# Scaling the exponentials of a banded attention before they are turned, in place of the output after it

## The chip, the cores and the metric

The kernel runs on one core of a Trainium2 chip. The metric is the device time of one execution in microseconds. An execution under the profiler leaves a trace, and the views below are read from it.

## The reference, cut to what matters

```python
def _attn_ref(q, k, v, n_global, n_local):          # q, k, v: (4, 8, 768, 64)
    scores = scale * np.matmul(q, k.transpose(0, 1, 3, 2)) + bias
    scores = np.where(keep, scores, -1e9)            # 8 global keys, 96 local ones
    scores = scores - np.max(scores, axis=-1, keepdims=True)
    a = np.exp(scores)
    a = a / (np.sum(a, axis=-1, keepdims=True) + 1e-09)
    return np.matmul(a, v)

def _moe_ref(x, w_gate, w1, w2):                     # x: (3072, 512), the attention's output
    ...                                              # gate: exp of logits, 8 rounds of row and column scaling
    for e in range(8):
        out += P[:, e:e + 1] * (np.maximum(x @ w1[e], 0.0) @ w2[e])
```

The quotient `a / sum` is what the change computes in another place. Everything is float32; the kernel splits large operands into a high and a low part and multiplies three products for one.

## The kernel before, in words

The program has two stages. In the first, some 325 us long, the attention is computed for 32 **pairs** of heads (`n`; 4 batches by 2 halves of the sequence by 4 pairs). Four pairs make a **unit**; there are eight. A pair has three **groups** (`t = 3n + group`), each a query tile of 128 rows for both heads. Behind it, for some 1870 us, the experts run as large matmuls, in a form with seven products in place of eight.

`Banded.unit` steps through a unit two groups at a time. One such step is called a **chunk** here, six to a unit. The chunk writes TensorE's (PE's) instructions in this order, and PE keeps it:

1. `ahead`: scores of the two groups that come four groups later (`s_ps`), then `softmax` of them: VectorE (DVE) adds the bias and takes the row maximum into `p_sb` (L309), ScalarE (ACT) takes the exponential in place and the row sums (L313).
2. `flush`: the product with V (`o_ps`) of the two groups that were turned in the chunk before. When a pair ends here, `o_ps` is multiplied by `inv` on DVE (L404), and split into the parts `xh` (ACT, L405) and `xl` (DVE, L406) that the experts read.
3. `turn`, twice: PE transposes the exponentials of two groups into `t_ps`, and a copy takes them to `pT` (L336).
4. `between`: some 4 us of **filler**, the first expert's matmuls on units that are done (`h_ps`, `y_ps`, `g_ps`).
5. In two chunks of three `prepare`: PE transposes q and k of a later pair into two `tp` tiles; ACT casts them to `qh` and `kh` (L266), DVE subtracts to `ql` and `kl` (L267). In the third chunk `invert`, for two pairs: PE transposes `inv` into `r_ps`, and DVE copies that back to `inv` (L414).

The sums are handled by pair: after the third group ACT adds EPS to the six sums (L316), DVE takes reciprocals (L317), and ACT spreads each over 64 columns into the tile `inv` (L319).

From the second unit on, `t_ps`, `tp` and `r_ps` share two PSUM banks (tag `tp`), given out in turn: the first `t_ps` of a chunk takes the bank of the q transposes before it, the second that of the k transposes, once `ql` and `kl` have been read out of them. `s_ps` has one bank for each head of the pair.

GpSimd (POOL) adds and subtracts x tiles for the later stage (L607 to L611, tile `op`). All DMAs are issued in one queue on SyncE (SP): the loads of q, k and v (`raw_qk`, `raw_v`, `early`), and the spills of what POOL made (`op_m<-op`, L817). On PE and SP, as on the others, a scheduler that runs when the program is built fixes one order, except that the attention's and filler's PE instructions stay as written. The wait of an instruction holds up all that stands behind it on its engine or queue.

Of the kernel before, what the change touches and what calls it, by code (L numbers as in the profile page):

```python
# [8 lines left out]
F32 = mybir.dt.float32  # L9
# [3 lines left out]
ALU = mybir.AluOpType  # L13
# [4 lines left out]
P = 128  # L18
# [4 lines left out]
EPS = 1e-9  # L23
UT = 3
# [8 lines left out]
CHUNK = 2  # L33
LAG = 6
FG = 2
GROUPS = (((0, 0), (1, 0)), ((0, 1), (1, 1)), ((0, 2), (1, 2)))
# [78 lines left out]
class Banded:  # L115
# [154 lines left out]
    def scores(self, ts):  # L270
# [19 lines left out]
                    self.pe.matmul(s_ps, lhsT=t[m][0], rhs=t[m][1], start=(m == 0), stop=(m == 2))  # L290
        return s_lists

    def softmax(self, t, s_list):


        nc, D = self.nc, self.D
        n, group = divmod(t, len(GROUPS))
        _, half, g = self.work[n]
        p_sb = self.wrk.tile([P, 2, 2, P], F32, name="p_sb")
        mx = self.wrk.tile([P, 2], F32, name="mx", bufs=4)  # L300
        if group == 0:
            self.sums[n] = self.wrk.tile([P, UT, 2], F32, name="sm", bufs=4)
        sm = self.sums[n]
        views = []
        for u, (j, i) in enumerate(GROUPS[group]):
            h = 2 * g + j
            pv = p_sb[:, u, 0:len(KEYS[half][i])]
            views.append(pv)
            nc.vector.tensor_tensor_reduce(out=pv, in0=s_list[u], in1=self.bias(h, half, i), scale=-(D ** -0.5), scalar=3.0e38,  # L309
                                           op0=ALU.add, op1=ALU.min, accum_out=mx[:, u:u + 1])  # L310
        for u, pv in enumerate(views):
            j, i = GROUPS[group][u]
            nc.scalar.activation(out=pv, in_=pv, func=AF.Exp, bias=mx[:, u:u + 1], scale=-1.0,  # L313
                                 accum_out=sm[:, i, j:j + 1])
        if group == len(GROUPS) - 1:
            nc.scalar.add(sm, sm, EPS)  # L316
            nc.vector.reciprocal(out=sm, in_=sm)  # L317
            self.inv[n] = self.wrk.tile([P, UT, P], F32, name="inv", bufs=3)
            nc.scalar.copy(out=self.inv[n].rearrange("p t (j d) -> p (t j) d", j=2),  # L319
                           in_=sm.rearrange("p t j -> p (t j)").unsqueeze(2).broadcast_to([P, 2 * UT, D]))  # L320
        return p_sb
# [31 lines left out]
    def unit(self, u, xh, xl, between):  # L353

        NG, per = len(GROUPS), len(GROUPS) * (self.H // 2)
        if u == 0:
            self.load_qk(1)
            self.prepare(0)  # L360
            self.scale_bias(0)
            self.keep_warm(self.ps, "o", WARM0)
            self.ahead(range(0, CHUNK))
            self.load_v(2)
            self.prepare(1)
            for g in range(1, self.H // 2):
                self.scale_bias(g)
            for t in range(CHUNK, AHEAD, CHUNK):
                self.ahead(range(t, t + CHUNK))
            self.prepare(2)  # L370
        for t in range(u * per, (u + 1) * per, CHUNK):
            self.ahead(range(t + AHEAD, t + AHEAD + CHUNK))
            self.flush()
            for t1 in range(t, t + CHUNK):
                n, group = divmod(t1, NG)
                if group == 0:
                    self.outs[n] = self.ps.tile([P, UT, P], F32, name="o_ps", tag="o", bufs=2)
                g = n % (self.H // 2)
                self.pending.append((n, group, self.turn(t1), self.outs[n], xh[g], xl[g]))
            for c in (CHUNK, 1, 1):  # L380
                between(c)
            n = t // NG
            if t % (2 * NG) == CHUNK:
                self.invert(n)
                self.invert(n + 1)
            else:
                self.prepare(n + NG)
        self.idle = None

    def flush(self):  # L390


        ended = None
        for n, group, pT, o_ps, xh, xl in self.pending:
            self.values(n, group, pT, o_ps)
            if group == len(GROUPS) - 1:
                ended = n, o_ps, xh, xl
        self.pending = []
        if ended is None:
            return  # L400
        n, o_ps, xh, xl = ended
        if n % 2:
            self.load_v(n + 3)
        self.nc.vector.tensor_tensor(out=o_ps, in0=o_ps, in1=self.inv.pop(n), op=ALU.mult)  # L404
        self.nc.scalar.copy(out=xh, in_=o_ps)  # L405
        self.nc.vector.tensor_tensor(out=xl, in0=o_ps, in1=xh, op=ALU.subtract)  # L406

# [683 lines left out]
```

## Time and profile before

| | before |
|---|---|
| median of 3 runs | 2198.84 us (2198.79 to 2199.56) |
| the profiled execution's own time | 2199.65 us |
| its span, first to last instruction | 2197.9 us |
| PE busy | 2177.2 us, 99% of the span |
| DVE, ACT, POOL busy | 1329.1, 757.1, 1127.9 us |

The profile is of one execution; 1.75 us of its time lie outside the span. Busy matmuls are pipelined and overlap in the records, so a row's mean duration is longer than what one costs PE; the cost is the step from one start to the next.

### The profile page before, as it was taken

The page shows a single profiled execution, that of the slowest core. Times are in us where ns is not written, and L with a number is a line of the kernel's source. Part 1 is how long each engine was busy: PE and PEld are TensorE (multiplying, and loading weights), DVE is VectorE, ACT ScalarE, POOL GpSimd, SP SyncE. Part 2 cuts the span into 40 slices and gives each one's busy share as a digit, 9 for nine tenths or more (in the row PEclk, how much of TensorE's full clock was granted, in tenths as well). Part 3 has the DMA queues.
Part 4 walks back from the last instruction along what each step waited for, and adds up shares of the span by engine and source line. Part 5 has one row for each costly group of instructions (what it writes and reads, how often), then busy time and mean ns, then how long its engine had stood idle before and what let it go on. Part 6 is the DMA issues. An engine that isn't in the chain of part 4 may idle for free.

```text
span 2197.9 us, 29372 instructions
## 1 busy us (share of the span) xinstructions
PE 2177.2 (99%) x10851; PEld 1811.4 (82%) x10851; DVE 1329.1 (60%) x2348; ACT 757.1 (34%) x1540; POOL 1127.9 (51%) x1061
## 2 busy tenths in 40 slices
PE   7999999999999999999999999999999999999998
PEld 5888888888888888888888888888888888888887
DVE  6555546756656666665665665665566566566565
ACT  6677763322222222223232222222232223222231
POOL 5767565445445445445455554544454545545440
PEclk8999999999999999999999999999999999999999
DMA  5666553111111111171111111111611111111111
GB/s 122 162 194 175 144 165 128 48 58 48 49 58 48 55 51 48 58 259 50 57 48 58 48 49 58 49 51 55 201 57 49 49 58 49 58 48 49 58 39 50
DMA packets 207817, 173.47 MB, mean 79 GB/s; under 512 B 102704, under 2 KB 170800, under 8 KB 207664
## 3 DMA queue, kind: packets, MB, share of 16 engines
q1 hardware_dynamic: 207664, 171.51, 25.3%
q8 instruction: 87, 1.43, 0.3%
q14 instruction: 66, 0.54, 0.1%
HBM read 142.36 MB, written 29.10 MB: 78 GB/s over the span
## 4 chain that ended last, share of the span: by engine, by line
PE 97%; ACT 1%; DVE 1%; DMA 0%; SPq 0%; issue 0%; POOL 0%; ACTq 0%; DVEq 0%
PE y_ps L109 46%; PE bank_a L109 11%; PE bank_d L109 11%; PE bank_c L109 11%; PE bank_b L109 5%; PE h_ps L109 3%; PE o_ps L109 2%; PE s_ps L109 2%; PE t_ps L112 2%; PE tp L112 1%; PE r_ps L112 1%; PE g_ps L109 0%; ACT p_sb L313 0%; PE y_ps L705 0%; PE y_ps L704 0%; PE y_ps L703 0%
## 5 line engine op out<-in xcount | busy, mean ns | idle before, releaser
L990 DVE SCALAR_TENSOR_TENSOR early<-y_ps,pm,early 128x512 f32<-128x512 f32 x672 | 503.0, 749 | 241.8 <-PE y_ps L109 241.3
L563 POOL TENSOR_TENSOR wl<-wsum,wh 128x1280 fp32r<-128x1280 f32 x90 | 266.2, 2957 | 577.8 <-ACT wh L562 577.8
L585 POOL TENSOR_TENSOR wsum<-w1f 128x256 f32<-128x256 f32 x450 | 317.5, 740 | 319.1 <-DMA w1f<-in_moe_w_dram 319.1
L109 PE MATMUL y_ps<-w2h,h_set 128*128 128x512 f32 x1408 | 433.5, 389 | 0.0
L109 PE MATMUL y_ps<-w2h,x 128*128 128x512 f32 x1408 | 433.4, 389 | 0.0
L562 ACT CAST w2h<-w2f 128x1024 fp32r<-128x1024 f32 x90 | 94.8, 1054 | 688.6 <-issue 610.6
L109 PEld LDWEIGHTS y_ps<-w2h,h_set 128*128 128x128 f32 x1408 | 264.3, 188 | 54.9
L109 PEld LDWEIGHTS y_ps<-w2h,x 128*128 128x128 f32 x1408 | 264.3, 188 | 54.9
L109 PE MATMUL y_ps<-w2l,h_set 128*128 128x512 f32 x704 | 274.1, 389 | 0.1
L109 PE MATMUL y_ps<-w2l,x 128*128 128x512 f32 x704 | 273.9, 389 | 0.0
L109 PE MATMUL bank_a<-m,wh 128*128 128x512 f32 x696 | 242.8, 389 | 1.0 <-DVE h_set L635 1.0
L109 PE MATMUL bank_d<-x,wh 128*128 128x512 f32 x696 | 242.7, 389 | 0.0
L109 PE MATMUL bank_c<-x,wh 128*128 128x512 f32 x696 | 242.5, 389 | 0.0
L563 POOL TENSOR_TENSOR w2l<-w2f,w2h 128x1024 fp32r<-128x1024 f32 x90 | 216.0, 2400 | 48.5 <-ACT w2h L562 48.5
L675 DVE TENSOR_TENSOR early<-early,bank_d 128x512 f32<-128x512 f32 x90 | 62.0, 689 | 175.8 <-PE bank_d L109 171.8
L109 PEld LDWEIGHTS y_ps<-w2l,h_set 128*128 128x128 f32 x704 | 132.1, 188 | 27.8 <-DVE early L990 0.5
L109 PEld LDWEIGHTS y_ps<-w2l,x 128*128 128x128 f32 x704 | 132.1, 188 | 27.5
L109 PEld LDWEIGHTS bank_a<-m,wh 128*128 128x128 f32 x696 | 130.6, 188 | 29.0 <-DVE h_set L635 1.9
L109 PEld LDWEIGHTS bank_c<-x,wh 128*128 128x128 f32 x696 | 130.6, 188 | 27.1
L109 PEld LDWEIGHTS bank_d<-x,wh 128*128 128x128 f32 x696 | 130.6, 188 | 27.1
L109 PE MATMUL bank_a<-m,wl 128*128 128x512 f32 x348 | 135.4, 389 | 0.0
L109 PE MATMUL bank_d<-x,wl 128*128 128x512 f32 x348 | 135.4, 389 | 0.0
(233 smaller groups left out, 3480.8 us busy)
## 6 DMA issues: line engine op xcount, KB each, us to landing
w1f<-in_moe_w_dram SPq DMA_DIRECT2D x92, 512.0 KB, 3.5
w2f<-in_moe_w_dram SPq DMA_DIRECT2D x92, 512.0 KB, 3.4
x<-op_m SPq DMA_DIRECT2D x16, 512.0 KB, 7.6
op_m<-op SPq DMA_DIRECT2D x30, 256.0 KB, 2.8
m<-op_m SPq DMA_DIRECT2D x12, 512.0 KB, 7.2
out_dram<-early SPq DMA_DIRECT2D x24, 256.0 KB, 4.0
ys<-y_sb SPq DMA_DIRECT2D x21, 256.0 KB, 2.8
early<-ys SPq DMA_DIRECT2D x21, 256.0 KB, 4.1
```

Source lines behind the costliest of these rows:

```text
L109: return self.tc.keep_in_program_order(self.engine.matmul(*args, **kw))
L112: return self.tc.keep_in_program_order(self.engine.transpose(*args, **kw))
L562: self.nc.scalar.copy(out=hi, in_=full)
L563: self.nc.gpsimd.tensor_tensor(out=lo, in0=full, in1=hi, op=ALU.subtract)
L585: nc.gpsimd.tensor_tensor(out=s[:, n], in0=x, in1=y, op=op)
L675: tt(out=t3, in0=t3, in1=d, op=ALU.subtract)
L990: nc.vector.scalar_tensor_tensor(out=a, in0=y_ps, scalar=moe.pm[:, tt, e:e + 1], in1=a, op0=ALU.mult, op1=ALU.add)
```

## The change

For pairs 0 to 3 (`early_pair`) all stays. For the other 28, each group takes its two sums into a small tile of its own, adds EPS and takes reciprocals on DVE, and multiplies the exponentials in `p_sb` by them: in the first and third group one head on DVE and one on ACT, in the second both on ACT. `invert` with its transposes, the spread tile `inv` and the multiplication of `o_ps` are dropped for these pairs.

```diff
+    def early_pair(self, n):
+
+        return n < self.H // 2
...
-        if group == 0:
+        early = self.early_pair(n)
+        if not early:
+            sm = self.wrk.tile([P, 2], F32, name="sm2", bufs=8)
+        elif group == 0:
             self.sums[n] = self.wrk.tile([P, UT, 2], F32, name="sm", bufs=4)
-        sm = self.sums[n]
...
-                                 accum_out=sm[:, i, j:j + 1])
-        if group == len(GROUPS) - 1:
+                                 accum_out=self.sums[n][:, i, j:j + 1] if early else sm[:, u:u + 1])
+        if not early:
+            nc.vector.tensor_scalar(out=sm, in0=sm, scalar1=EPS, scalar2=None, op0=ALU.add)
+            nc.vector.reciprocal(out=sm, in_=sm)
+            for u, pv in enumerate(views):
+                if u == 0 and group != 1:
+                    nc.vector.tensor_scalar(out=pv, in0=pv, scalar1=sm[:, u:u + 1], scalar2=None, op0=ALU.mult)
+                else:
+                    nc.scalar.mul(pv, pv, sm[:, u:u + 1])
+        elif group == len(GROUPS) - 1:
+            sm = self.sums[n]
             nc.scalar.add(sm, sm, EPS)
             nc.vector.reciprocal(out=sm, in_=sm)
-            self.inv[n] = self.wrk.tile([P, UT, P], F32, name="inv", bufs=3)
+            self.inv[n] = self.wrk.tile([P, UT, P], F32, name="inv", bufs=2)
...
-            if t % (2 * NG) == CHUNK:
+            if t % (2 * NG) != CHUNK:
+                self.prepare(n + NG)
+            elif self.early_pair(n):
                 self.invert(n)
                 self.invert(n + 1)
-            else:
-                self.prepare(n + NG)
...
-        self.nc.vector.tensor_tensor(out=o_ps, in0=o_ps, in1=self.inv.pop(n), op=ALU.mult)
+        if self.early_pair(n):
+            self.nc.vector.tensor_tensor(out=o_ps, in0=o_ps, in1=self.inv.pop(n), op=ALU.mult)
```

Three places of the built order, before and now. The first is on PE, in the second unit, at the end of an `invert` chunk: filler (`h_ps`), the transposes of `inv` (`r_ps`), and the next chunk's scores. Before:

```order
L109 MATMUL h_ps<-x_194,w1h 128x384
L109 MATMUL h_ps<-x_192,w1l 128x384
L109 MATMUL h_ps<-x_192,w1h 128x384
L112 MATMUL r_ps<-ident,inv 128x128 x6
L109 MATMUL s_ps_1054<-kl,qh 128x256
L109 MATMUL s_ps_1055<-kl,qh 128x256
```

Now:

```order
L109 MATMUL h_ps<-x_194,w1h 128x384
L109 MATMUL h_ps<-x_192,w1l 128x384
L109 MATMUL h_ps<-x_192,w1h 128x384
L109 MATMUL s_ps_1073<-kl,qh 128x256
L109 MATMUL s_ps_1074<-kl,qh 128x256
```

The six transposes are gone here and at 13 more places; nothing else on PE moves, and the scores follow the filler.

The second is on DVE, at the 24th `prepare` (the one whose q transposes start at 211.07 us in the trace before): the subtractions `ql` and `kl` that free the two `tp` banks, and the four maxima (`ISA`, each with a read of its result) of the chunk behind them. Before:

```order
L406 TENSOR_TENSOR x_195<-o_ps,x_193 128x3x128
L317 RECIPROCAL sm<-sm 128x6
L267 TENSOR_TENSOR ql<-tp,qh 128x384
L267 TENSOR_TENSOR kl<-tp,kh 128x512
L309 ISA p_sb,mx<-s_ps_3505,early 128x256
L309 ISA mx 128x1
```

Now:

```order
L326 TENSOR_SCALAR p_sb<-p_sb,sm_3504 128x256
L267 TENSOR_TENSOR ql<-tp,qh 128x384
L315 ISA p_sb,mx<-s_ps_3589,early 128x256
L315 ISA mx 128x1
L315 ISA p_sb,mx<-s_ps_3589,early 128x256
L315 ISA mx 128x1
L315 ISA p_sb,mx<-s_ps_3590,early 128x256
L315 ISA mx 128x1
L315 ISA p_sb,mx<-s_ps_3590,early 128x256
L315 ISA mx 128x1
L267 TENSOR_TENSOR kl<-tp,kh 128x512
```

`kl` has moved behind the four maxima. It stands so at the 16th, 24th and 32nd `prepare`, and at no other from the third unit on. At the same place ACT's order ahead of the `qh` and `kh` casts was

```order
L405 CAST x_193<-o_ps 128x3x128
L862 COPY y_sb<-y_ps 128x512
L316 ACTIVATE sm<-sm 128x6
L266 CAST qh<-tp 128x384
L319 COPY inv<-sm 128x384
L266 CAST kh<-tp 128x512
```

and is now

```order
L351 COPY pT<-t_ps 128x512
L328 ACTIVATE p_sb<-p_sb,sm_3493 128x256 x2
L877 COPY y_sb<-y_ps 128x512
L328 ACTIVATE p_sb<-p_sb,sm_3504 128x256
L266 CAST qh<-tp 128x384
L266 CAST kh<-tp 128x512
```

Three scalings (L328) have come between; the EPS addition and the spread copy are gone, and the cast of x (L420 now) stands further ahead.

The third is on SP, at the loads of q and k for the 16th `prepare`. Before:

```order
L218 DMA raw_qk<-in_k_dram 32x2x64
L218 DMA raw_qk<-in_k_dram 96x2x64 x2
L218 DMA raw_qk<-in_k_dram 32x2x64
L218 DMA raw_qk<-in_k_dram 96x2x64
L218 DMA raw_qk<-in_k_dram 32x2x64
L817 DMA op_m_204<-op 256x1x512
L218 DMA raw_qk<-in_k_dram 128x2x64
```

Now:

```order
L218 DMA raw_qk<-in_k_dram 32x2x64
L218 DMA raw_qk<-in_k_dram 96x2x64 x2
L832 DMA op_m_204<-op 256x1x512
L218 DMA raw_qk<-in_k_dram 32x2x64
L218 DMA raw_qk<-in_k_dram 96x2x64
L218 DMA raw_qk<-in_k_dram 32x2x64
L218 DMA raw_qk<-in_k_dram 128x2x64
```

The spill of POOL's result has moved ahead of three loads; the last load (`128x2x64`) stands behind the same DMAs as before. At the 12th `prepare` the same kind of spill has moved ahead of two.

## Rows read from the trace of the kernel before

**Rows 1.** The page: share by engine of the chain that ended last.

```profile
PE 97%; ACT 1%; DVE 1%; DMA 0%; SPq 0%; issue 0%; POOL 0%; ACTq 0%; DVEq 0%
```

**Rows 2.** By stretch: PE, PEld, DVE, ACT, POOL busy (x), PEclk, DMA share, GB/s.

```profile
80.00:120.00 40.00, 38.87 (x331) 33.68 (x327) 20.84 (x79) 27.60 (x88) 38.04 (x39) 1.00 0.64 178
120.00:160.00 40.00, 40.00 (x343) 35.08 (x343) 21.53 (x78) 28.73 (x88) 25.39 (x31) 1.00 0.64 173
```

**Rows 3.** Waits of PE over the span, the longest: us, times, longest one.

```profile
PE s_ps L109 <- DVE kl L267: 4.3, 2, 3.2
```

**Rows 4.** Tile inv: ns min/median/max, first and last start, forms.

```profile
L414 DVE COPY inv<-r_ps x32: 546/557/559, 31.2 to 316.8; 128x384 f32<-128x384 f32 x32
L319 ACT COPY inv<-sm x32: 497/513/525, 21.9 to 309.5; 128x384 f32<-128x384 f32 x32
...
L404 DVE TENSOR_TENSOR o_ps<-o_ps,inv x32: 555/561/567, 34.0 to 322.4; 128x384 f32<-128x384 f32 x32
```

**Rows 5.** PE in order of time (start, us), at chunk ends with and without r_ps.

```profile
138.96 0.34 PE L109 MATMUL h_ps<-x,w1h 128*128 128x384 f32 x1
139.14 0.82 PE L112 MATMUL r_ps<-ident,inv 128*128 128x128 f32 x6
139.89 0.39 PE L109 MATMUL s_ps<-kl,qh 64*128 64x256 f32 x2
...
303.96 0.34 PE L109 MATMUL h_ps<-x,w1h 128*128 128x384 f32 x1
304.22 0.39 PE L109 MATMUL s_ps<-kl,qh 64*128 64x256 f32 x2
```

**Rows 6.** By line, near the added operations: ns min/median/max, first and last start.

```profile
L989 ACT ACTIVATE early<-early,pm x24: 711/722/727, 416.4 to 1631.4; 128x512 f32<-128x512 f32 x24
...
L317 DVE RECIPROCAL sm<-sm x32: 179/181/193, 21.7 to 309.3; 128x6 f32<-128x6 f32 x32
...
L190 DVE TENSOR_SCALAR bias<-early x2: 452/536/621, 11.8 to 12.5; 128x128 f32<-128x128 f32 x2
L190 DVE TENSOR_SCALAR early<-early x2: 414/583/752, 12.1 to 12.6; 128x512 f32<-128x512 f32 x2
```

**Rows 7.** PE, then ACT, then DVE in order of time, around the 24th prepare.

```profile
211.07 0.93 PE L112 MATMUL tp<-ident,raw_qk 128*128 128x128 f32 x7
211.93 0.39 PE L109 MATMUL s_ps<-kl,qh 64*128 64x256 f32 x2
...
213.86 1.09 PE L112 MATMUL t_ps<-ident,p_sb 128*128 128x128 f32 x8
...
211.60 0.48 ACT L266 CAST qh<-tp 128x384 fp32r<-128x384 f32 x1 [0.33 <-PE tp L112]
...
213.01 0.69 DVE L267 TENSOR_TENSOR kl<-tp,kh 128x512 fp32r<-128x512 f32 x1 [0.34 <-ACT kh L266]
```

**Rows 8.** PE, then DVE, in a chunk whose maxima waited for the scores.

```profile
199.18 0.39 PE L109 MATMUL s_ps<-kl,qh 64*128 64x256 f32 x2
...
200.20 0.43 DVE L309 CUSTOM_DVE_ANT_1 p_sb<-s_ps,early 128x256 f32<-128x256 f32 x1 [0.21 <-PE s_ps L109]
...
200.54 0.42 DVE L309 CUSTOM_DVE_ANT_1 p_sb<-s_ps,early 128x256 f32<-128x256 f32 x1
```

**Rows 9.** PE at the 12th prepare, SP ahead of the 16th, PE at the 16th.

```profile
93.20 0.33 PE L112 MATMUL tp<-ident,raw_qk 128*128 128x128 f32 x1 [1.13 <-DMA raw_qk<-in_k_dram]
...
111.97 2.53 SPq L232 DMA_DIRECT2D early<-in_q_dram  x2
...
127.64 1.39 SPq L817 DMA_DIRECT2D op_m<-op  x1
129.08 0.61 SPq L218 DMA_DIRECT2D raw_qk<-in_k_dram  x1
...
131.87 1.15 PE L112 MATMUL tp<-ident,raw_qk 128*128 128x128 f32 x7
132.95 0.39 PE L109 MATMUL s_ps<-kl,qh 64*128 64x256 f32 x2
```

## The prediction

> **What bounds the kernel now.** I read the chain that ended last first: 97% of it is PE [rows 1], so a microsecond counts only if it is PE's. Next the busy time by stretch, because the change touches the attention alone (up to some 325 us): from 120 us on PE is busy for 40.00 of 40 us, with ACT at 28.7 and DVE at 21.5, at a granted clock of 1.00 [rows 2], the higher of its two levels (2.4 GHz). Then PE's waits: the longest kind in the whole run is 4.3 us, two waits for `kl` [rows 3]. So in this stage every transpose that PE no longer makes can be gained, as long as no new wait takes its place. The reader is to see both halves: PE has no slack, and ACT and DVE have 28% and 46%, which says nothing yet of when they are late.
>
> **What PE saves.** The 84 transposes into `r_ps` go, in 14 runs of six. With them a filler matmul started at 138.96 and the next chunk's scores at 139.89, 0.93 us later; without them (a chunk near the end) 303.96 and 304.22, 0.26 us [rows 5]. So a run is worth 0.67 us, less than the six rows' own length, since the switch from filler to scores costs a little either way. 14 x 0.67 = 9.4 us. That is the ceiling.
>
> **What is lost ahead of the 16th prepare.** Four of the 14 runs lie there, one in each half unit of some 20 us. But at two places the loads of q and k are late already: at the 12th prepare PE waited 1.13 us for the last load of k, and at the 16th the transposes took 1.08 us up to the scores (131.87 to 132.95) where the same seven took 0.86 at the 24th (211.07 to 211.93) [rows 7, 9]. SP was issuing without a gap of over 0.1 us from 111.97 until that load at 129.08 [rows 9], and POOL was busy for 38.04 of 40 us from 80 on [rows 2]; neither gets work taken from it. So PE can come earlier to the 16th prepare and will wait there for the same load: 4 x 0.67 = 2.7 us are not gained. The bounds are 0 (SP itself moves up) and 2.7; I take 2.7, since the queue's rows show it full. That the spill now stands three loads further ahead costs nothing by itself: the last load of k has the same DMAs in front of it.
>
> **What kl costs.** At three prepares, the 16th, 24th and 32nd, DVE now subtracts `kl` behind the next chunk's four maxima, and the second `t_ps` needs the bank that `kl` empties. At the 24th: scores from 211.93. Maxima started 1.02 us after the first score where they waited for nothing else (199.18, 200.20), and step by 0.34 [rows 8]. So they run from 212.95 to 214.33, and `kl`, 0.69 long [rows 7], to 215.02. `t_ps` started at 213.86 and its second half some 0.5 us in, at 214.36 [rows 7]. PE waits 0.66 us where it waited for nothing. If ACT is late it is more: three scalings now stand ahead of `qh`. The nearest row is the same operation on 512 columns, 0.722 us [rows 6]; for 256 that bounds it by 0.36 and 0.72, and I take 0.5, some 0.4 of it not overlapped. 1.2 us, less 0.1 for the EPS addition and 0.33 for which ACT was idle there [rows 7], makes `qh` 0.8 late; `ql` and the maxima then start at about 213.4, and the wait is 1.1. Bounds 0.66 and 1.1, taken 0.8, as PE's own lateness at the 16th gives ACT time back: 3 x 0.8 = 2.4 us.
>
> **What lies beside PE.** ACT gets 112 scalings (12 on 128 columns) of some 0.5 us and loses 28 spread copies of 0.513 [rows 4] and 28 smaller additions: some 35 us more, so about 33 of 40 where it had 28. DVE loses 28 copies at 0.557, 28 products at 0.561 [rows 4] and 28 reciprocals at 0.181, 36 us, and gets 84 reciprocals and 84 EPS additions of the same small kind (at 0.18 each, 30 us), and 56 scalings. For these the nearest rows are fixed multiplications from SBUF to SBUF: 0.414 and 0.752 on 512 columns, 0.452 and 0.621 on 128 [rows 6]. Bounds 0.2 (half of 0.414) and 0.75, taken 0.45, as three of the four rows lie nearer to that than to 0.2: 25 us. At the other prepares the cover is this: `kl` ended at 213.70 and its bank was wanted at 214.36, 0.66 us later; `ql`'s bank has some 1.2 us [rows 7]. ACT is some 0.4 to 0.8 us later there, since the dropped spread copy often stood ahead of `qh`. I take the cover to hold; without it each of 22 prepares would lose 0.1 to 0.3 us (a rival below). `o_ps` loses a step between PE and ACT; nobody waited for it. New scalings behind an exponential have a whole chunk, some 6.6 us, until their group is turned. Waits that the first of the new work brings ahead of 93 us go into the 1.13 us for which PE waits at 93.20 anyway [rows 9].
>
> **The sum.** 9.4 - 2.7 - 2.4 = 4.3 us. The profiled execution took 2199.65 us, 1.75 outside the span; it would take 2195.3. The median of the runs is 0.8 us lower, so 2198.84 - 4.3 = **2194.5 us**. A measurement of this kernel can tell about 0.2%, 4.4 us, so the forecast lies almost on that line.
>
> **DVE and POOL.** Two of the four rows of DVE's multiplications are longer than the other size allows: 128 columns took 0.452 and 0.621 where 512 took 0.414 [rows 6]; something held them up by 0.2 to 0.4 us. The Trainium skill, page "SBUF — State Buffer", section "Who interferes with whom", has a reason: a VectorE copy or scalar operation that may use two ports and a GpSimd instruction exclude each other for a whole instruction. In the rows it shows as a few tenths, not as a full stop. By the rule taken whole the time would be that of the slower rival; by the rows, half of it is in the 0.45 above.
>
> **Rivals.** (1) Less is lost: SP moves up with PE, or `kl` comes in time. Without the waits for `kl` 6.7 us are gained, without any loss 9.4: 2192.1 to 2189.4 us. For it: the queue's order changed at the 16th prepare, and 0.66 us is small against one reading of where the maxima may start. Against it: the built order itself puts `kl` last. (2) ACT is late at the other prepares too, as its queue rises by a sixth: 22 x 0.1 to 0.2 us, 3 us less: 2197.5 us, no change that can be told. For it: cover of 0.66 against lateness of up to 0.8; against it: before, ACT still had idle time ahead of `qh` at the place read. (3) Slower: DVE is held up by POOL at each new operation. A chunk has two additions and 1.3 scalings; if each is held by 0.34 (0.752 less 0.414), `kl` is 1.1 us later in every chunk, 0.5 beyond its cover; 22 x 0.5 = 11 us are lost for 4.3 gained: 2205.5 us. It decides from a mean new wait of 0.2 us at each prepare on, where the gain is gone. For it: POOL is busy for 25 to 38 of 40 us [rows 2]; against it: additions of two columns are over soon, and most of DVE's new work stands behind the maxima, when DVE is idle for ACT.
>
> **Chances.** Forecast 0.5 (own range 2192.5 to 2196.5, half on each side of the 0.2% line), rival 1 0.2, rival 2 0.2, rival 3 0.1. Faster by over 0.2%: 0.2 and half of 0.5, 0.45. Slower by over 0.2%: 0.1. Within: 0.45. The range 2190.0 to 2200.5 us leaves out the far half of rival 1 and most of rival 3, under 0.2.
>
> **What would show it.** In the profile of the changed kernel: `r_ps` with 12 matmuls; scores 0.26 us behind filler at the `invert` chunks; a wait of PE for a load of `raw_qk` near 130 us that takes up what was won until then; three waits of `t_ps` for `kl` of 0.7 to 1.1 us, some 79 us apart; PE else at 40.00 of 40. The prediction is wrong if PE waits for `kl` or `ql` at many prepares, if the DVE scalings take over 0.75 us, if no wait for the load is seen, or if the later stage, whose order does not change, differs in length.

## The result and the profile after

The changed kernel takes 2209.28 us (median of 6 runs, 2206.92 to 2211.0), the kernel before in the same comparison 2199.15 (2198.73 to 2199.78): a ratio of 1.0045, interval 1.0032 to 1.0058. It is slower by 10 us, on the side of the third rival, and outside the range. The profiled execution took 2209.38 us with a span of 2207.2.

The chain that ended last shows PE at 92% where it had 97% [rows 1]:

```profile
PE 92%; DVE 3%; ACT 3%; issue 1%; DMA 1%; SPq 0%; POOL 0%; ACTq 0%; DVEq 0%
```

Busy time by stretch, in the columns of [rows 2], and two stretches of 20 us:

```profile
80.00:120.00 40.00, 37.74 (x305) 32.19 (x302) 31.41 (x95) 29.72 (x93) 36.63 (x37) 0.96 0.64 175
120.00:160.00 40.00, 38.30 (x325) 32.73 (x324) 29.30 (x101) 31.92 (x94) 25.93 (x32) 1.00 0.61 171
...
40.00:60.00 20.00, 15.19 (x143) 11.75 (x140) 19.12 (x58) 14.87 (x46) 10.24 (x7) 0.91 0.64 158
100.00:120.00 20.00, 17.74 (x129) 15.30 (x128) 15.74 (x46) 13.99 (x45) 19.29 (x16) 0.91 0.65 184
```

PE now stands still for 2.3 and 1.7 of 40 us where it stood for 1.1 and for none, and DVE went from 21 to some 30 us of them. Over the whole run DVE is busy for 1382.4 us, 53.3 more than before, where the prediction's own figures (30 and 25 us given, 36 taken) make 19. In the two stretches of 20 us the granted clock is 0.91, where it was 1.00 in both before: PE had stopped there and worked a while at the lower of its two levels afterwards.

PE's waits over the span, and ACT's between 40 and 325 us (us, times, longest):

```profile
PE t_ps L112 <- DVE kl L267: 5.5, 4, 1.9
PE tp L112 <- issue: 4.3, 2, 2.1
PE s_ps L109 <- DVE kl L267: 4.2, 2, 3.2
PE tp L112 <- DMA raw_qk<-in_k_dram: 2.1, 2, 1.4
...
ACT p_sb L328 <- DVE sm L323: 13.2, 14, 2.3
```

The old kind of [rows 3] is still there with 4.2 us. New are `t_ps` behind `kl`, two waits of `tp` for which the profile names no releaser, and ACT standing for 13.2 us at its scalings until DVE's reciprocal is there.

The added lines (ns min/median/max, first and last start, forms):

```profile
L322 DVE TENSOR_SCALAR sm<-sm x84: 149/225/1941, 43.5 to 317.5; 128x2 f32<-128x2 f32 x84
...
L323 DVE RECIPROCAL sm<-sm x84: 149/165/169, 45.5 to 318.0; 128x2 f32<-128x2 f32 x84
...
L326 DVE TENSOR_SCALAR p_sb<-p_sb,sm x56: 285/591/2217, 45.7 to 318.2; 128x256 f32<-128x256 f32 x44, 128x128 f32<-128x128 f32 x12
...
L328 ACT ACTIVATE p_sb<-p_sb,sm x112: 400/508/542, 45.7 to 319.5; 128x256 f32<-128x256 f32 x100, 128x128 f32<-128x128 f32 x12
```

Two columns take a reciprocal 0.165 us every time; the addition of EPS to the same two columns takes between 0.149 and 1.941. The timeline shows what decides. DVE, POOL, ACT and PE in order of time, where the change begins (POOL splits the first expert's weights into `w1l` and `w2l` here):

```profile
43.49 1.94 DVE L322 TENSOR_SCALAR sm<-sm 128x2 f32<-128x2 f32 x1
45.47 0.17 DVE L323 RECIPROCAL sm<-sm 128x2 f32<-128x2 f32 x1
45.67 2.20 DVE L326 TENSOR_SCALAR p_sb<-p_sb,sm 128x256 f32<-128x256 f32 x1
...
47.86 0.55 DVE L429 COPY inv<-r_ps 128x384 f32<-128x384 f32 x1
...
43.05 2.36 POOL L588 TENSOR_TENSOR w1l<-w1f,w1h 128x1024 fp32r<-128x1024 f32 x1
45.37 2.35 POOL L588 TENSOR_TENSOR w2l<-w2f,w2h 128x1024 fp32r<-128x1024 f32 x1
...
45.73 0.51 ACT L328 ACTIVATE p_sb<-p_sb,sm 128x256 f32<-128x256 f32 x1 [1.64 <-DVE sm L323]
48.51 0.91 ACT L328 ACTIVATE p_sb<-p_sb,sm 128x256 f32<-128x256 f32 x2 [2.28 <-DVE sm L323]
...
48.46 0.67 PE L112 MATMUL tp<-ident,early 128*128 128x128 f32 x4 [1.21 <-DVE inv L429]
```

POOL's subtraction ends at 45.41, DVE's addition at 45.43; POOL's next at 47.72, DVE's scaling at 47.87. The reciprocal between them ran beside POOL for its usual time. Over the whole stage 41 additions and 38 scalings took over 0.12 us more than their usual 0.16 and 0.34, 45 us in all, about half on each. Every one of these additions ended 0.02 to 0.03 us, every one of the scalings 0.08 to 0.15 us, behind the end of a POOL instruction; of the others none began while a POOL instruction had 0.3 us still to run. 33 of the 84 reciprocals lie wholly within one, and none was longer. Of the 13.2 us for which ACT stood at its scalings, some 6.6 lie within held time. For the rest DVE was at other operations ahead of the reciprocal, and how late those were through earlier holds is not shown.

The second place is the gate's transposes `gt_ps`, a fourth user of the two banks of the tag `tp`. DVE, then PE:

```profile
107.78 0.67 DVE L322 TENSOR_SCALAR sm<-sm 128x2 f32<-128x2 f32 x1 [0.33 <-ACT p_sb L319]
108.56 1.12 DVE L322 TENSOR_SCALAR sm<-sm 128x2 f32<-128x2 f32 x1
109.60 1.44 DVE L326 TENSOR_SCALAR p_sb<-p_sb,sm 128x256 f32<-128x256 f32 x1
...
111.15 1.17 DVE L326 TENSOR_SCALAR p_sb<-p_sb,sm 128x128 f32<-128x128 f32 x1
...
112.44 0.18 DVE L753 TENSOR_TENSOR lg<-gt_ps,lg 128x24 f32<-128x24 f32 x1
...
110.09 0.49 PE L112 MATMUL tp<-ident,early 128*128 128x128 f32 x3
112.73 1.08 PE L112 MATMUL tp<-ident,early 128*128 128x128 f32 x4 [2.15 <-issue]
...
115.31 1.49 PE L109 MATMUL o_ps<-pT,early 128*64 128x128 f32 x16
```

POOL runs its instructions of 1.3 us back to back, and DVE gets one such operation in at the end of each: four of them take from 107.78 to 112.32. The reader of `gt_ps` stands behind, and PE's transposes of k start 0.11 us after it. The profile says "issue"; that the bank is the releaser is read from these two times, here and in the same way at 195.70. After this stop the clock is at the lower level: sixteen `o_ps` take 1.49 us where they take 1.09 at the higher one. After the like stop at 195.70 it is not: between 180 and 200 us the granted clock is 1.00.

DVE needs 4.46 us from the first of these additions to the first reader of `gt_ps` (107.78 to 112.24). The version without the additions (no_eps below) has the same reciprocals and scalings there and needs 2.35, and PE has no wait:

```profile
101.11 0.17 DVE L322 RECIPROCAL sm<-sm 128x2 f32<-128x2 f32 x1 [0.33 <-ACT p_sb L319]
...
103.46 0.17 DVE L751 COPY lg<-gt_ps 128x24 f32<-128x24 f32 x1
...
103.51 1.10 PE L112 MATMUL tp<-ident,early 128*128 128x128 f32 x7
```

The following sets the same PE work of both traces side by side: the start of the chunk's first scores before, and how much later or earlier it is in some of the kernels (the later ones are explained below).

| start before | after | no_eps | after_8 | late_half | no_scale |
|---|---|---|---|---|---|
| 44.66 | -0.5 | -1.1 | -0.3 | -0.4 | -0.8 |
| 59.15 | +6.6 | -0.4 | -0.4 | +0.5 | -0.9 |
| 100.13 | +4.1 | -2.3 | -2.5 | -1.9 | -2.8 |
| 119.98 | +7.6 | -2.8 | -1.3 | -2.4 | -3.5 |
| 179.33 | +7.9 | -3.7 | +0.1 | -3.4 | -5.0 |
| 199.18 | +10.0 | -4.1 | +3.6 | -4.1 | -5.7 |
| 298.17 | +9.3 | -5.2 | +3.1 | -6.4 | -9.3 |

The loss is not spread over the prepares: 7.1 us fall between 44.66 and 59.15, 3.5 between 100 and 120, 1.4 between 133 and 147, 2.1 between 179 and 199, net of what the dropped transposes give back. At 304.22, near the end of the stage, the changed kernel is 9.3 us late, and its span is 9.3 us longer (2207.2 and 2197.9): the later stage takes as long as before.

### The profile page after: what moved, and what is told of

The parts are those of the page before. It is cut to its first block, busy times and chain, and to the rows that moved or that the text cites. A ratio compares the mean times of both kernels' runs of the same rounds, so it can differ in the third digit from the quotient of the medians.

```text
span 2207.2 us, 29407 instructions
## 1 busy us (share of the span) xinstructions
PE 2174.0 (98%) x10767; PEld 1803.9 (82%) x10767; DVE 1382.4 (63%) x2488; ACT 785.5 (36%) x1596; POOL 1128.5 (51%) x1061
## 4 chain that ended last, share of the span: by engine, by line
PE 92%; DVE 3%; ACT 3%; issue 1%; DMA 1%; SPq 0%; POOL 0%; ACTq 0%; DVEq 0%
PE y_ps L109 45%; PE bank_a L109 11%; PE bank_d L109 11%; PE bank_c L109 11%; PE bank_b L109 5%; PE h_ps L109 2%; ACT p_sb L319 1%; PE t_ps L112 1%; PE s_ps L109 1%; PE o_ps L109 1%; PE tp L112 1%; DVE p_sb L315 1%; DVE p_sb L326 0%; DVE sm L322 0%; ACT p_sb L328 0%
```

## The experiments

The theory: some of DVE's operations that read and write SBUF wait until the POOL instruction that is running ends, and what stands behind them, ACT's scalings and the readers of PE's banks, is late (A). The rivals: DVE and ACT simply have too much work (B), or `kl` behind the maxima costs the time (C). All times are medians with the ratio to the kernel before and its interval, measured on the same chip.

**no_eps.** The additions alone are taken out of the program.

```diff
-            nc.vector.tensor_scalar(out=sm, in0=sm, scalar1=EPS, scalar2=None, op0=ALU.add)
             nc.vector.reciprocal(out=sm, in_=sm)
```

> The 84 EPS additions on DVE are left out for pairs 4 to 31; the order on all engines and the scalings stay. A sum of exponentials of scores less their maximum is at least 1, so the addition of 1e-9 changes nothing in float32. Theory A (DVE's multiplications and additions from SBUF to SBUF wait until POOL's running instruction ends, and what stands behind them is late): 22.9 of the 45.0 us by which DVE's new operations were held go, the scalings' 22.1 us stay; some half of the 10 us comes back, 2202 to 2206 us, and reciprocals stay at 0.165 us. Theory B (DVE and ACT simply have too much work): 84 x 0.16 us of 70 us less on DVE, 2208 to 2209. Theory C (kl behind the maxima costs the time): its place does not change, 2209.

2194.24 us, 0.9977 (0.9968 to 0.9986): all that was lost comes back, and the kernel is faster than before. ACT's waits for reciprocals, 13.2 us in the changed kernel, are 0.3. The scalings are still held, 31 of 56, by 16.1 us in all:

```profile
L325 DVE TENSOR_SCALAR p_sb<-p_sb,sm x56: 286/532/1383, 43.2 to 303.2; 128x256 f32<-128x256 f32 x44, 128x128 f32<-128x128 f32 x12
```

The size was missed: theory A had put half of the loss on the scalings. They are held and cost little; without the additions the kernel is 15 us faster. `kl` stands behind the maxima as before, so C falls as the main cause. B does not fall by this run alone: the additions are also 84 x 0.16 = 13 us of plain work. And the order did not stay as was expected. In the traces DVE's differs at three places between 44 and 59 us, and ACT's there and at ten places behind them, at seven of which a scaling stands further ahead. The runs pool_free and late_add, which keep the order of the kernel that each is compared with, tell more.

**act_scales and both.** All scalings go to ACT (`if u == 0 and group != 1` and its branch are dropped), with the additions and without.

> The 56 scalings go from DVE to ACT, which makes all 168; the EPS additions stay on DVE. Theory A: the 22.1 us for which scalings were held go, the additions' 22.9 stay: 2202 to 2206 us. Theory B: ACT, which gets 56 x 0.5 = 28 us more, is later still: 2211 or more. Theory C: kl's place at three prepares changes, and 1 to 4 us come back: 2205 to 2208.

2220.71 us, 1.0099 (1.0083 to 1.0114): slower, as B had it.

> EPS additions left out for pairs 4 to 31 and all scalings on ACT: DVE keeps the reciprocals alone of the new work. Theory A: nothing of DVE is held, the 8.6 us that PE saves are kept but for late casts of ACT: 2191 to 2196 us, faster than before. Theory B: 2209 or more, since ACT has 28 us more than in the changed kernel. Theory C: 2205 to 2208.

2210.93 us, 1.0055 (1.0042 to 1.0069), although nothing of DVE's new work can be held:

```profile
PE t_ps L112 <- DVE ql L267: 10.7, 9, 1.3
```

Theory A forecast a gain in both of these runs and was wrong. B gave the direction, but ACT's load is not what PE waits for. The built order changed with the edit: in both traces `ql` stands behind one to four of the next chunk's maxima at twelve prepares from the 9th on, and `kl` behind all four, where in the changed kernel `kl` alone does so at three. At each of the nine waits for `ql` in `both`, the cast `qh` had ended 0.7 to 1.2 us before `ql` began, and DVE had no idle time ahead of it. ACT and DVE at one of them:

```profile
157.09 0.48 ACT L266 CAST qh<-tp 128x384 fp32r<-128x384 f32 x1
...
158.35 0.42 DVE L315 CUSTOM_DVE_ANT_1 p_sb<-s_ps,early 128x256 f32<-128x256 f32 x1
...
158.70 0.55 DVE L267 TENSOR_TENSOR ql<-tp,qh 128x384 fp32r<-128x384 f32 x1
...
159.40 1.09 PE L112 MATMUL t_ps<-ident,p_sb 128*128 128x128 f32 x8 [1.29 <-DVE ql L267]
```

So these two runs show theory C's mechanism at more places, and what 28 us more on ACT cost by themselves they do not show. Between the two the additions make 9.8 us; DVE's order is the same in both but for one reciprocal, ACT's differs in the place of some copies of `pT`.

**pool_free.** POOL's combining of x tiles is left out, and a tile of zeros is spilled in the place of each result.

```diff
+        still = xout.tile([P, 2, 2, KH, P], F32R, name="op")
+        nc.vector.memset(still.bitcast(F32), 0.0)
...
-            new = xout.tile([P, 2, 2, KH, P], F32R, name="op")[:, :, 0:n]
-            moe.combine((new[:, 0], new[:, 1]), block(x, c, n), block(y, c, n), op, xtmp)
-            spills.append((op_spill[b][m][:, :, q], new))
+            spills.append((op_spill[b][m][:, :, q], still[:, :, 0:n]))
```

> The changed kernel with POOL's additions and subtractions of x tiles in the attention stage left out; one tile of zeros is spilled in the place of each result, by the same DMAs, so the output is not the reference's. POOL's split of the first expert's weights (up to 65 us) stays. DVE's and ACT's work and order in the attention stage stay. Theory A: from 65 us on additions take 0.16 and scalings 0.35 us, the losses of PE behind 65 us (some 11 us, of which kl's place may keep 2 to 4) go, those of some 7 us between 42 and 58 us stay: 2200 to 2202 us. Theories B and C: 2209.

The durations answer clearly. Additions and scalings from 160 us on, where POOL does nothing in this kernel:

```profile
L322 DVE TENSOR_SCALAR sm<-sm x50: 161/169/172, 164.7 to 320.6; 128x2 f32<-128x2 f32 x50
...
L326 DVE TENSOR_SCALAR p_sb<-p_sb,sm x34: 285/353/355, 165.1 to 321.0; 128x256 f32<-128x256 f32 x26, 128x128 f32<-128x128 f32 x8
```

In the changed kernel the additions of that stretch reach 1.135 us and 21 of 48 are held; here none is. The time as a whole, 2216.01 us (1.0077, 1.0064 to 1.0091), is neither theory's number, because of what happens before 160 us. Spills that no longer wait for POOL run early (261 GB/s between 80 and 120 us, where the changed kernel has 175): nineteen stand on SP in a row, the spill of `y_sb` behind them, ACT waits 9.95 us for that to land, and PE 8.07 us at 118.86.

```profile
93.83 18.18 SPq L834 DMA_DIRECT2D op_m<-op  x19
...
115.62 0.59 ACT L877 COPY y_sb<-y_ps 128x512 f32<-128x512 f32 x1 [9.95 <-DMA ys<-y_sb]
...
118.86 0.50 PE L112 MATMUL gt_ps<-ident,g_sb 16*128 16x16 f32 x3 [8.07 <-ACT pT L351]
```

From 160 us on PE waits for no load in either kernel, and DVE and ACT do the changed kernel's work in its order (one copy of `y_sb` on ACT apart). There the run decides between A and B. Columns as in [rows 2], the changed kernel first, then this one:

```profile
160.00:200.00 40.00, 37.73 (x321) 32.18 (x320) 28.45 (x94) 30.16 (x94) 21.12 (x17) 1.00 0.54 149
...
160.00:200.00 40.00, 39.97 (x341) 34.27 (x341) 22.71 (x98) 32.00 (x98) 0.00 (x0) 1.00 0.55 138
```

Between the scores at 160.42 and those at 298.17 of the kernel before, the changed kernel loses 1.2 us against it, this one wins 2.4, and no_eps wins 2.1. The additions that are not held cost nothing there that can be told, so in that stretch it is the holds and not the work.

**two_input.** The same two operations on DVE with two tensor inputs (`self.eps` is a tile that is set to EPS once).

```diff
-            nc.vector.tensor_scalar(out=sm, in0=sm, scalar1=EPS, scalar2=None, op0=ALU.add)
+            nc.vector.tensor_tensor(out=sm, in0=sm, in1=self.eps, op=ALU.add)
...
-                    nc.vector.tensor_scalar(out=pv, in0=pv, scalar1=sm[:, u:u + 1], scalar2=None, op0=ALU.mult)
+                    nc.vector.tensor_tensor(out=pv, in0=pv, in1=sm[:, u:u + 1].unsqueeze(2).broadcast_to(list(pv.shape)), op=ALU.mult)
```

> The changed kernel with the same additions and scalings on DVE in another form: the EPS addition adds a tile that holds EPS, the scaling multiplies by the sums' tile read along the row, so that both have two tensor inputs in SBUF in place of one and a scalar. Order and counts stay. Theory A1 (only the one-input forms wait for POOL): additions at 0.16 to 0.2 us, scalings at 0.35 to 0.45, none held; 2192 to 2196 us. Theory A2 (forms with two inputs in SBUF wait for POOL as well): some 40 additions and 38 scalings held, 2207 to 2212. Theory B (work): 2209.

2209.61 us, 1.0044 (1.003 to 1.0057): the time of the changed kernel, as A2 had it. 51 additions and 35 scalings are held, by 26.7 and 24.8 us:

```profile
L324 DVE TENSOR_TENSOR sm<-sm,eps x84: 146/407/1279, 44.0 to 322.4; 128x2 f32<-128x2 f32 x84
...
L328 DVE TENSOR_TENSOR p_sb<-p_sb,sm x56: 291/722/2357, 45.6 to 323.4; 128x256 f32<-128x256 f32 x44, 128x128 f32<-128x128 f32 x12
```

So another form with both inputs in SBUF is no way out, while the maxima of 256 columns (one input in PSUM) stay at 0.42 us on average in this kernel and in the changed one.

**before_adds and before_recips.** To the kernel before 84 additions are added that nobody reads, or 84 reciprocals in the same places.

```diff
+        if n >= self.H // 2:
+            nc.vector.tensor_scalar(out=mx, in0=mx, scalar1=EPS, scalar2=None, op0=ALU.add)
```

> The kernel before with one more DVE addition of EPS (a tile of 128x2, the row maxima that nobody reads any more) behind the exponentials of each group of pairs 4 to 31, 84 in all; nothing is removed. Theory A: some 40 of them are held until a POOL instruction ends, 20 to 27 us of DVE's time; slower than the sister kernel with reciprocals in their place by 2 us or more, 2202 to 2212. Theory B: 84 x 0.16 us on DVE, which has slack: 2199 to 2200, like its sister.

2199.59 us, 1.0002 (0.9993 to 1.0011). Theory A's time was wrong, its hold right: 36 of the additions are held, 20.6 us in all.

```profile
L316 DVE TENSOR_SCALAR mx<-mx x84: 154/218/2196, 43.3 to 308.0; 128x2 f32<-128x2 f32 x84
```

> The same kernel with a reciprocal of 128x2 in the place of each of the 84 additions; the order of all engines is the same. Theory A: none is held, 0.165 us each, 2199 to 2200.5 us. Theory B: the same as its sister with additions.

2199.51 us, 1.0002 (0.9993 to 1.0011). In the kernel before, held additions cost nothing that can be told.

**no_scale.** No additions and no scalings for the 28 pairs.

> The changed kernel without EPS additions and without any scaling for pairs 4 to 31 (reciprocals stay), so the output is not the reference's: what PE saves with next to nothing put beside it. kl stands ahead of the maxima at all prepares from the eighth on. If the loads take back what is saved ahead of the 16th prepare (2.7 us of 9.4): 2192 to 2193 us, with waits of PE for loads near 90 and 130 us. If they move up with PE: 2190 to 2191.

2191.29 us, 0.9965 (0.9951 to 0.9978), between the two numbers. The lags of the chunks tell more: at 139.89 this kernel is 3.7 us ahead of the kernel before, five runs of transposes at 0.66 and 0.4 more. At the 16th prepare PE does wait for the load of k, and its lead falls from 3.46 us (at 126.25) to 3.06 (at 132.95): the loads take back 0.4, not 2.7.

```profile
129.39 0.57 PE L112 MATMUL tp<-ident,raw_qk 128*128 128x128 f32 x2 [0.28 <-DMA raw_qk<-in_k_dram]
```

**first_add and late_add.** To no_eps one unread addition is added per group, ahead of the reciprocal or behind the scalings.

```diff
+            nc.vector.tensor_scalar(out=mx, in0=mx, scalar1=EPS, scalar2=None, op0=ALU.add)
             nc.vector.reciprocal(out=sm, in_=sm)
```

> The version without EPS additions (2194.2 us), with one DVE addition that nobody reads (on the row maxima, 128x2) put ahead of each reciprocal of pairs 4 to 31: DVE's order is that of the changed kernel. Theory A' (a held addition delays the reciprocal behind it, and ACT, which keeps its order, stands at its scaling until the reciprocal is there): nobody needs the addition's result, but what stands behind it in DVE's queue is as late as in the changed kernel: 2207 to 2211 us, and ACT waits for reciprocals for 10 us or more in all. Theory A'' (the real addition costs because its result is needed): 2194 to 2197.

2205.2 us, 1.0026 (1.0015 to 1.0037), below A' and far above A'': 11 of the 15 us, though nobody needs the sum. ACT's order differs from that of no_eps at four places, and the other 4 us are not explained. ACT's waits for reciprocals:

```profile
ACT p_sb L328 <- DVE sm L323: 12.3, 11, 2.0
```

> The same additions put behind the group's scalings in the program. They are as many and are held as long (20 to 27 us of DVE's time). Theory A': ACT's scalings no longer wait for them: 2194 to 2198 us. Theory A''' (DVE's time is what counts, wherever it goes): 2205 to 2211.

2201.49 us, 1.0009 (1.0 to 1.0019), between the theories' numbers. The additions are held as long (23.9 us against 21.7), and ACT's waits halve, since now only an addition of the group before can stand ahead:

```profile
ACT p_sb L327 <- DVE sm L322: 6.3, 6, 3.0
```

DVE's and ACT's order is that of no_eps, the additions apart, so these 7 us are theirs alone. So the place in DVE's queue counts, not the sum that is added: the same 84 held additions cost nothing in the kernel before, 7 us behind the scalings, 11 ahead of the reciprocals.

**eps_act.** The addition on ACT, `nc.scalar.add(sm, sm, EPS)`.

> The changed kernel with the EPS addition of each group on ACT in place of DVE (0.2 us each, 17 us more on ACT); kl stands behind one to four of the maxima at every second prepare. Theory A alone: 2194 to 2198 us, since no addition is held. Theory B' (ACT, busy for 33 of 40 us, is late for the casts at the prepares, as where it made all scalings): 2200 to 2208, with waits of t_ps for ql and kl.

2198.3 us, 0.9995 (0.9986 to 1.0004). It lies between the numbers of the two theories. No addition is held; PE waits for `kl` eleven times:

```profile
PE t_ps L112 <- DVE kl L267: 5.9, 11, 1.4
```

At ten of them the cast was done and DVE was at the maxima that the built order puts ahead of `kl`, so it is again the order that makes `kl` late, and not shown that ACT does.

**half_dve.** no_eps with one scaling on DVE and one on ACT in each group (`if u == 0:`).

> The version without EPS additions, with one scaling on DVE and one on ACT in all three groups (84 and 84 in place of 56 and 112). kl stands ahead of the four maxima at the 16th, 24th and 32nd prepare. Theory C (kl's place is what is left of the loss in the version without additions: waits of 3.5 us): 2190 to 2192 us, no wait of t_ps for kl there. Theory A: 28 more scalings held by 0.3 us or so on DVE eat part of it: 2192 to 2195. If DVE becomes late at the other prepares: 2197 or more.

2194.16 us, 0.9975 (0.9965 to 0.9986), the time of no_eps by another sum. `kl` stands ahead of the maxima and `t_ps` no longer waits for it, but between 44.66 and 59.15 us, where more scalings on DVE meet POOL's long instructions, it goes from 0.6 us ahead of the kernel before to 2.5 behind.

**after_8.** The changed kernel, beginning with pair 8 (`return n < self.H`, three tiles `inv`).

> The changed kernel with pairs 4 to 7 left as in the kernel before too (the change begins with pair 8, two tiles inv more in place of one), additions and scalings of the rest unchanged. If the 7.5 us lost between 42 and 58 us come from DVE's new work meeting POOL's split of the first expert's weights (2.4 us an instruction there): that loss goes and two of PE's savings (1.3 us) with it, 2202 to 2205 us, the losses behind 100 us stay. If the early loss only moves to the first pairs of the change: 2207 to 2211.

2202.3 us, 1.0014 (1.0005 to 1.0023). The early loss is gone and does not come again where the change now begins; the later ones stay (table). So it goes with the stretch in which POOL's instructions take 2.4 us.

**late_half and half8.** no_eps with half the scalings on DVE from pair 8 on, and half_dve beginning with pair 8.

> No EPS additions; pairs 4 to 7 scaled as in the changed kernel (two of six scalings of a pair on DVE), pairs 8 to 31 with three on DVE and three on ACT. By the lags of the two versions that it joins (the one without additions has -0.4 us at 59 us, the one with half the scalings on DVE wins 7.6 us more behind that place): 2190 to 2192 us, below both. If DVE's held scalings take it back: 2194.

2193.08 us, 0.9972 (0.9962 to 0.9983), between its two forecasts: the lowest of the versions that leave out no scaling, faster than both kernels; its interval overlaps with that of no_eps. `t_ps` waits for `kl` once, 0.9 us.

> No EPS additions, half the scalings on DVE, and the change beginning with pair 8. PE saves 12 runs of transposes of 0.66 us, 7.9, and nothing meets POOL's split of the weights: 2191 to 2193 us. If the early loss moves to the first pairs of the change: 2194 to 2196.

2193.95 us, 0.9977 (0.9968 to 0.9986), at the lower end of its second forecast: no different from the others that can be told.

## Why the prediction was wrong

**What lies beside PE** is the step that failed. It priced the EPS additions like the reciprocals, "of the same small kind" at 0.18 us each, and the scalings at 0.45 with bounds 0.2 and 0.75. The additions measured 0.43 on average and up to 1.94, the scalings 0.73 and up to 2.22. With that "I take the cover to hold" fell: ACT stood 13.2 us at its scalings, and the banks of `tp`, `gt_ps` among them, came free late. The third rival had this mechanism and even the mean hold (0.34 taken; 0.27 for an addition and 0.4 for a scaling measured), at a chance of 0.1. Its place was wrong: it lost 0.5 at each of 22 prepares, while the trace loses most in three places in which several holds follow one another; at two of them PE then runs at the lower clock as well. And the two reasons given against it do not hold: "additions of two columns are over soon" looked at the operation's own length, when it is POOL's that counts, and behind the maxima DVE is not idle but what ACT waits for.

The Trainium skill's rule, page "SBUF — State Buffer", section "Who interferes with whom", was set aside because four rows showed tenths. The runs agree with it taken whole: a scalar operation of DVE waits until the running GpSimd instruction has ended (a scaling up to 2.22 us in place of 0.34), and an operation with two inputs in SBUF does so too (51 of 84 held in two_input). The four rows misled in part because only DVE's side of them was read. With POOL's beside it, in the kernel before:

```profile
11.53 1.49 POOL L190 TENSOR_SCALAR early<-early 128x512 f32<-128x512 f32 x1
...
12.48 0.62 DVE L190 TENSOR_SCALAR bias<-early 128x128 f32<-128x128 f32 x1
```

POOL's ends at 13.02 and DVE's at 13.10, 0.08 us behind it, which is where the held scalings of 128 columns end in the changed kernel (0.08 behind). So the 0.621 can be a full hold until the end of an instruction that had 0.5 us left. The two operations ahead of it (0.452 and 0.414) ran within the same instruction; why they were not held stays open.

**What PE saves** was right: `r_ps` is down to two runs, scores follow filler within 0.27 us (104.01 and 104.28), and between 219 and 278 us, where nothing new waits, the changed kernel wins back 0.5 to 0.7 us at each dropped run.

**What is lost ahead of the 16th prepare** was wrong in size: 2.7 us taken, 0.4 measured (no_scale), near its other bound of 0. SP moves up with PE: the `raw_qk` loads for the 16th prepare are issued from 121.47 us on in no_scale, from 122.97 before.

**What kl costs** was right in its mechanism and, without the additions, in its size: 2.4 us taken for the three prepares, 0.64, 0.98 and 0.98 measured in no_eps. In the changed kernel it is 1.33, 1.29 and 0.97; half_dve, where `kl` stands ahead there, has no such wait. The sum left out a fourth place: at the 8th prepare `kl` stands behind four maxima too, and PE waits 0.91 us there in no_eps and 1.87 in the changed kernel.

**The sum** of 2194.5 us is what no_eps takes (2194.24), which is partly luck. At 298.17 no_scale is 9.3 us ahead, the loads' loss already in it, and no_eps 5.2; 3.5 of the 4.1 between them are the four waits for `kl`. So the loads' loss, 2.3 too high, made up for a fourth wait that was not counted and for smaller losses. What separates no_eps from 2209.3 is the additions, and with them ACT's order at a few places.

**The second rival** (ACT late) is not seen in any run: no_eps has the same scalings on ACT and gains. At the waits for `ql` in `both`, and at ten of eleven for `kl` in eps_act, the cast was done before DVE came to the subtraction.

## What to carry to other kernels

Before a DVE addition or multiplication from SBUF to SBUF is put beside a busy POOL, price it by the length of POOL's instructions, not by its own, and look at which in-order queue stands behind it; the held time cost nothing where nobody waited (before_adds). A tiny operation can cost more than a large one: here the kernel is 15 us faster without 84 additions of two columns, and only some 3 us faster again without the 168 scalings (no_scale). A variant that moves work can move the built order too, so its order is read before its time is laid to the work. An addition that cannot change the result (1e-9 to a sum of at least 1 in float32) is better dropped than moved.

## What the runs showed of the hardware that was not expected

- Which operations wait for POOL: TENSOR_SCALAR and TENSOR_TENSOR with all inputs in SBUF, even on two columns; RECIPROCAL from SBUF to SBUF never (0.165 us, 33 of 84 beside a running POOL instruction).
- DVE gets in at the end of each POOL instruction, even when POOL's follow back to back: between 107.78 and 112.32 us a run of held operations advances by one in 1.3 us.
- POOL's own busy time did not grow: 1128.5 us after, 1127.9 before.
